# A new issue order for a fused attention and wave-MLP kernel, with 78 copies on other engines and filler products on TensorE

## The chip, the core and the metric

The kernel runs on one core of a Trainium2 chip. The metric is the device time of one execution in microseconds; three executions of the kernel before gave 228.94 (median), 229.01 and 228.08. A further execution was profiled, and all rows of the trace are from that one.

## What is computed

For each of 8 batches, 8 heads of 576 positions by 64 channels go through a linear attention with a root-mean-square norm, and the heads side by side (576 by 512) go through a wave MLP:

```python
kv = np.einsum('bhsd,bhse->bhde', k, v)
out = np.einsum('bhsd,bhde->bhse', q, kv)
x = out / np.sqrt(np.mean(out * out, axis=-1, keepdims=True) + 1e-06) * g_norm
theta = x @ w_theta                                   # x now (8, 576, 512)
y = w_tok_r @ (x * np.cos(theta)) + w_tok_i @ (x * np.sin(theta))
u = x + y
return u + np.maximum(u @ w_ch, 0.0)
```

Inputs and output are float32; the products run in float16 with sums in float32, but for batch 0's k-v product, which is taken in float32.

## The kernel before

A batch's 576 rows are cut into four full tiles of 128 rows (j = 0 to 3) and a tail of 64 rows, which is folded to 128 partitions by 256 columns (names ending in e). `plan()` (line 41) makes a list of 1205 numbered tasks, each with a kind, an engine and arguments; a string of numbers, `TURNS` (line 144), says in which order the tasks are issued, for all engines together. Each engine works through its own share strictly in that order, and semaphores that follow from the tiles' readers and writers make it wait. So `TURNS` sets two things: what stands behind what on each engine, and through this when a buffer comes free.

The tasks of one batch, in the order in which the data goes through them:

- **Loads.** `ldm` and `ldt` bring k and v (rows and tail) into three `stage` buffers in turn: batch 0's k has stage 0, its v stage 1, batch 1's k stage 2, batch 1's v stage 0 again. They are issued on SP (batch 0's v on ACT). `lq` and `lqe` bring q on POOL's queue, and its DMA casts to float16. `lw`, `lwe` (token weights, POOL), `lwth` (w_theta, SP) and `lwch` come once. `hold` (L331) is a copy of one element on POOL that waits until a part of k has landed, and so keeps back what POOL issues after it.
- **k-v product.** `ca` casts k and v to float16 (L365 on ACT for k, L367 on POOL for v); `kv` multiplies (L396; `kv32`, L377, for batch 0), `ko` copies the result into `kbd` (L269 on ACT, L273 on DVE).
- **Attention.** q is turned, for batches 0 and 1 on TensorE (`qt`, L412, and the copy `qo`), later by the DMA (`qd`, `qde`). `raw` is the product with `kbd` (L446, L455); `sq` squares on ACT (L466), `ss` sums on DVE (L475), `rt` takes the power -0.5 on POOL (L481), `x` scales on DVE (L493, L503).
- **Angle.** `xt` turns x on TensorE (L412), `xo` copies it out on ACT with the factor of g (L271), `th` multiplies with w_theta (L520, L527), `pt`, `arg`, `abs` reduce the angle (ACT L543, DVE L548, L555), `sin` and `cos` run on ACT (L563, L569), `z` multiplies on DVE (L583). `zmv` moves the tail's z on SP's queue (L589).
- **Token mixing.** `y` and `ye` multiply z with the turned token weights, in three parts (L605, L614). The weights are turned once, in nine tiles, by `wt` on TensorE (L352, L353) and copied out by `wo`; `wth` scales and casts w_theta.
- **Channel mixing.** `us`, `um` add x (DVE L619, L627), `ut` turns u (L412), `uo` copies it (L269), `v` multiplies with w_ch (L520, L527), `fin` joins both on DVE (L664), `st`, `ste` store on SP's queue.

TensorE's results stand in PSUM tiles of three tags: `tr` (two buffers) for what is turned, `raw` (two), `acc` (four) for the other products. Words of `TURNS` like `r18` are `idle(tag, n)` (L681): n filler products of 128 by 512 into a tile of that tag, whose result nobody reads. Before, there are two: `r18` and `r9`, both before 13 us.

Of the kernel before, what the change touches and what calls it, by code (L numbers as in the profile page):

```python
# [18 lines left out]
P = 128  # L19
# [125 lines left out]
5 1 8 0 4 9 r18 80 81 3 6 r9 66 67 16 52 44 53 2 45 7 13 12 46 47 11 15 68 69 14 73 59 54 55 70 71  # L145
72 48 56 74 49 60 50 57 34 51 30 10 82 35 38 83 31 58 26 84 39 186 61 62 19 85 27 42 18 36 17 63 86
43 64 75 40 37 65 76 28 22 24 41 29 184 183 32 77 25 33 78 123 21 23 187 124 96 97 87 125 88 79 126
127 190 98 189 193 99 185 114 115 105 188 100 106 89 191 194 200 90 199 197 128 101 91 116 196 107
192 92 195 102 117 337 103 336 108 104 93 204 338 198 205 201 94 118 119 202 129 211 203 232 95 109
206 212 218 130 207 213 120 131 214 121 208 136 110 111 209 233 480 140 215 216 481 122 137 139 135  # L150
210 112 134 225 234 113 219 226 133 346 217 487 235 236 145 141 132 220 339 493 239 240 248 249 146
237 150 151 20 142 335 496 221 351 238 138 275 155 144 222 276 157 147 490 143 152 149 154 342 343
340 227 356 349 345 348 148 277 158 241 344 278 242 153 223 352 279 174 483 347 224 228 159 243 350
280 175 250 353 281 229 354 251 160 252 230 253 482 164 156 244 231 161 166 355 282 165 283 245 176
357 341 359 360 257 358 286 369 258 285 246 254 266 484 167 361 267 362 169 162 370 259 287 284 260
247 177 255 488 491 179 371 363 372 268 625 489 261 256 494 262 492 626 269 263 180 292 170 291 497
270 364 264 501 373 374 495 265 272 365 290 271 273 366 274 498 367 502 375 627 500 368 296 295 376
628 301 485 393 377 499 297 306 384 394 486 302 307 379 385 395 300 380 386 168 381 382 308 309 378
411 396 638 310 383 289 305 412 387 420 514 504 515 397 294 402 288 388 516 299 517 505 293 506 503
389 507 304 421 422 390 298 399 635 518 509 398 403 391 510 629 171 303 163 511 178 508 316 311 318  # L160
512 423 424 636 400 519 404 632 317 426 642 326 633 312 392 425 405 639 331 513 524 630 172 427 319
321 320 413 525 526 173 327 770 520 646 406 414 332 323 322 521 415 634 637 538 640 529 428 641 527
407 539 643 324 408 522 328 528 313 409 565 530 644 645 416 329 523 431 401 430 540 566 541 314 567
547 556 568 417 429 569 542 531 548 570 418 771 432 434 437 419 571 435 410 647 772 557 532 773 572
442 649 544 533 650 330 436 651 535 439 916 447 573 777 780 652 631 444 783 774 440 654 543 655 325
449 534 653 445 433 452 536 576 574 648 441 656 454 545 438 455 657 575 182 537 786 446 546 450 658
781 549 550 778 181 659 915 451 784 443 660 683 787 664 448 665 918 577 551 674 684 558 661 675 553
779 666 471 782 559 461 315 785 472 560 552 662 473 788 463 917 453 466 476 791 789 663 667 790 462
669 554 474 676 477 561 670 464 562 668 677 582 456 563 457 555 671 467 685 468 678 692 672 564 932
928 923 578 693 775 776 673 587 469 679 592 583 710 792 597 701 588 686 919 680 687 681 688 694 580  # L170
682 711 689 599 695 712 702 690 713 593 714 600 581 585 929 691 931 794 715 465 586 696 922 590 591
799 697 795 800 796 716 334 703 595 698 579 797 793 596 801 475 458 924 802 798 804 584 717 718 704
925 805 705 699 803 806 621 926 707 589 594 927 828 930 819 333 933 829 700 706 807 598 814 808 1062
719 820 720 611 936 470 613 809 606 459 708 934 612 622 722 721 935 815 816 810 817 601 821 614 607
1063 811 830 822 602 812 818 616 608 855 460 617 831 727 823 825 618 856 709 832 939 732 857 737 824
937 479 813 1061 826 609 846 837 940 725 847 941 742 744 1068 848 730 858 827 942 619 834 838 944
735 859 849 943 921 861 850 860 1071 945 833 862 740 863 724 1060 851 949 946 864 1066 920 1065 729
723 734 1064 835 938 728 852 950 866 951 726 947 733 615 731 1074 948 624 1077 738 853 1067 865 1070
1069 1073 745 736 739 952 954 836 955 478 1072 964 1076 610 620 741 1075 973 956 957 867 839 1078
1083 1081 965 603 974 953 959 756 840 1079 966 841 761 1080 758 958 960 843 743 757 961 967 604 762  # L180
991 975 746 842 962 605 844 753 992 751 759 968 963 747 976 1000 854 970 845 977 1104 1082 872 766
752 1001 877 754 767 1105 1002 1003 882 982 1084 1106 887 969 993 1004 1005 979 983 1085 971 1086
994 889 1107 748 755 1108 972 984 1145 1006 890 1089 995 1007 978 1090 868 1146 871 980 1087 749
1091 981 1008 1092 985 1088 873 876 986 1093 878 1147 1094 881 996 888 997 1011 987 870 1095 883 998
# [549 lines left out]
```

## Time and profile before

| what | value |
|---|---|
| median of three runs | 228.94 us (228.08 to 229.01) |
| the profiled execution | 226.97 us; its span from first to last instruction 225.2 us |
| granted TensorE clock, mean | 0.939 |
| PE busy | 204.8 us in 1629 matmuls |
| DVE busy | 166.5 us in 318 instructions |
| ACT busy | 157.1 us in 304 instructions |
| POOL busy | 108.6 us in 115 instructions |
| DMA | 40.82 MB, 181 GB/s over the span |

The busy time of an engine is the union of its instructions' durations; PE overlaps matmuls, so its busy time says that something was in the array, not that it streamed at its peak. The granted clock is the share of the full TensorE clock. Times in the trace's rows count from the first instruction.

### The profile page before, as it was taken

The numbers are of one execution on the slowest core, as the hardware profiler recorded it, in microseconds if no ns is written. First come the engines' busy times: TensorE is split into PE (matmuls) and PEld (weight loads), VectorE is DVE, ScalarE is ACT, GpSimd is POOL, SyncE is SP. The second block draws the span as 40 slices with busy tenths as digits, with TensorE's granted clock in tenths as the row PEclk, the third lists the DMA queues.
The fourth block names the chain that finished last, engine by engine and source line by source line (L and its number), as shares of the span: only waits on it lengthen the run. The fifth ranks groups of instructions, "written<-read, shape, count | busy, mean of one in ns | idle before, by whom it ended". The sixth has DMA issues, their size and how long they took to land.

```text
span 225.2 us, 4427 instructions
## 1 busy us (share of the span) xinstructions
PE 204.8 (91%) x1629; PEld 115.3 (51%) x1629; DVE 166.5 (74%) x318; ACT 157.1 (70%) x304; POOL 108.6 (48%) x115
## 2 busy tenths in 40 slices
PE   7497879589997999989999998899999999999993
PEld 3166654445654554654565445454656455445451
DVE  5003854685799889997899689897998997776363
ACT  2014288998999688989779886889699666644130
POOL 8022567048678567930884288359734506001000
PEclk9955755969999999999999999999999999999999
DMA  5999699499999897999989979985991122204145
GB/s 141 229 229 169 210 311 192 154 300 249 169 273 140 215 243 204 188 242 209 274 139 316 215 110 249 257 250 39 255 172 51 66 78 82 70 3 151 47 171 190
DMA packets 63252, 40.82 MB, mean 181 GB/s; under 512 B 29312, under 2 KB 58624, under 8 KB 63232
## 3 DMA queue, kind: packets, MB, share of 16 engines
q1 hardware_dynamic: 47216, 32.81, 56.0%
q0 software_dynamic: 14432, 6.57, 23.7%
q10 hardware_dynamic: 1584, 1.18, 1.9%
q8 instruction: 12, 0.20, 0.4%
q14 instruction: 8, 0.07, 0.1%
HBM read 33.10 MB, written 9.44 MB: 189 GB/s over the span
## 4 chain that ended last, share of the span: by engine, by line
PE 44%; DVE 18%; ACT 13%; DMA 11%; POOL 8%; issue 3%; SPq 1%; POOLq 0%; DVEq 0%; ACTq 0%
PE y L605 14%; PE v L520 7%; PE th L520 7%; POOL rt L481 6%; DMA qh<-in_q_dram 5%; DVE ss L475 4%; DMA out_dram<-ot 3%; DMA stage<-in_k_dram 3%; DVE arg L548 3%; DVE x L493 2%; PE ups L412 2%; PE ye L614 2%; PE xps L412 2%; PE wps L352 2%; DVE kbd L273 2%
## 5 line engine op out<-in xcount | busy, mean ns | idle before, releaser
L481 POOL TENSOR_TENSOR rt<-ss,mhalf 128x8 f32<-128x8 f32 x32 | 53.9, 1686 | 54.6 <-DVE ss L475 52.5
L605 PE MATMUL y<-wT,zm 128*128 128x512 f16 x256 | 63.6, 382 | 0.6 <-DVE ote L664 0.3
L605 PEld LDWEIGHTS <-zm 128*128 128x128 f16 x256 | 23.8, 98 | 26.0 <-issue 2.6
L520 PE MATMUL th<-wth,xTb 128*128 128x512 f16 x128 | 33.8, 392 | 0.0
L520 PE MATMUL v<-wch,uTb 128*128 128x512 f16 x128 | 31.7, 379 | 0.0
L619 DVE SCALAR_TENSOR_TENSOR uTb<-y,gcol,xTb 128x512 f16<-128x512 f32 x32 | 23.3, 746 | 9.7 <-PE y L605 9.6
L493 DVE TENSOR_TENSOR x<-raw,rt 128x512 f16<-128x512 f32 x32 | 22.0, 688 | 10.0 <-POOL rt L481 9.7
L269 ACT COPY ur<-ups 128x512 f16<-128x512 f16 x32 | 18.4, 591 | 10.3 <-PE ups L412 9.4
L475 DVE TENSOR_REDUCE ss<-sqb 128x8 f32<-128x520 f32 x32 | 21.8, 689 | 4.7 <-ACT sqb L466 4.6
L271 ACT ACTIVATE xTb<-xps,gcol 128x512 f16<-128x512 f16 x32 | 21.3, 686 | 5.4 <-PE xps L412 2.7
L466 ACT ACTIVATE sqb<-raw 128x512 f32<-128x512 f32 x32 | 19.0, 596 | 8.5 <-PE raw L446 7.1
L548 DVE SCALAR_TENSOR_TENSOR arg<-pt,th 128x512 f32<-128x512 f32 x32 | 21.7, 682 | 4.0 <-ACT pt L543 3.8
L664 DVE SCALAR_TENSOR_TENSOR ot<-v,ur 128x512 f32<-128x512 f32 x32 | 21.7, 684 | 3.5 <-DMA out_dram<-ot 1.4
L569 ACT ACTIVATE sc<-arg,quarter 128x512 f16<-128x512 f32 x32 | 22.9, 723 | 1.9 <-DVE arg L555 1.8
L543 ACT ACTIVATE pt<-th 128x512 f32<-128x512 f32 x32 | 19.3, 604 | 7.1 <-PE th L520 7.0
L583 DVE TENSOR_TENSOR zm<-x,sc 128x1024 f16<-128x1024 f16 x32 | 21.6, 687 | 2.1 <-ACT sc L569 2.1
L367 POOL CAST v<-stage 128x640 f16<-128x640 f32 x28 | 19.5, 719 | 5.2 <-DMA stage<-in_v_dram 5.2
L563 ACT ACTIVATE sc<-arg 128x512 f16<-128x512 f32 x32 | 20.0, 633 | 0.5 <-DVE arg L548 0.4
L365 ACT CAST k<-stage 128x640 f16<-128x640 f32 x28 | 19.3, 726 | 0.2 <-DMA stage<-in_k_dram 0.2
L520 PEld LDWEIGHTS <-xTb 128*128 128x128 f16 x128 | 11.7, 100 | 11.6 <-issue 1.6
L520 PEld LDWEIGHTS <-uTb 128*128 128x128 f16 x128 | 11.6, 98 | 10.9 <-issue 0.4
L273 DVE CAST kbd<-kv 64x256 f16<-64x256 f32 (+1 forms) x18 | 7.0, 388 | 12.7 <-PE kv L377 12.6
(85 smaller groups left out, 310.6 us busy)
## 6 DMA issues: line engine op xcount, KB each, us to landing
out_dram<-ot SPq DMA_DIRECT2D x32, 256.0 KB, 2.8
stage<-in_k_dram SPq DMA_DIRECT2D x7, 1024.0 KB, 6.9
stage<-in_v_dram SPq DMA_DIRECT2D x7, 1024.0 KB, 7.7
qh<-in_q_dram POOLq DMA_DIRECT2D x7, 512.0 KB, 6.7
stage<-in_k_dram SPq DMA_DIRECT2D x2, 512.0 KB, 7.2
stage<-in_k_dram SPq DMA_DIRECT2D x8, 128.0 KB, 5.7
stage<-in_v_dram ACTq DMA_DIRECT2D x2, 512.0 KB, 9.6
zm<-in_moe_w_theta_dram SPq DMA_DIRECT2D x1, 1024.0 KB, 6.3
```

Of the source, the lines that this page charges most:

```text
L271: nc.scalar.activation(out=dst, in_=src, func=AFT.Copy, scale=by)
L475: nc.vector.reduce_sum(out=ss[:], in_=live.pop(("sq", b, j))[:], axis=AXX)
L481: nc.gpsimd.tensor_tensor(out=rt[:], in0=live.pop(("ss", b, j))[:], in1=mhalf[:, 0:h], op=ALU.pow)
L493: nc.vector.tensor_tensor(out=live["xp", b, p][:, :, a * HC:(a + 1) * HC].rearrange("p t (h e) -> p h t e", e=D), in0=r[:].rearrange("p (h ...
L520: nc.tensor.matmul(t[:], lhs(kc), w[:, kc, :], start=(kc == 0), stop=(kc == NKC - 1))
L548: nc.vector.scalar_tensor_tensor(out=arg[:, 0, :], in0=live.pop(("pt", b, j))[:], scalar=MAGIC, in1=live.pop(("th", b, j))[:], op0=ALU.sub ...
L563: nc.scalar.activation(out=sc[:, 1, :], in_=live["arg", b, j][:, 0, :], func=AFT.Sin, bias=0.0, scale=-TURN * SHRINK,)
L569: nc.scalar.activation(out=live["sc", b, j][:, 0, :], in_=live.pop(("arg", b, j))[:, 1, :], func=AFT.Sin, bias=quarter[:], scale=-TURN * S ...
L583: nc.vector.tensor_tensor(out=dst, in0=x.unsqueeze(1).broadcast_to((P, 2, w)), in1=sc[:], op=ALU.mult)
L605: nc.tensor.matmul(t[:], r[:, c * P:(c + 1) * P], wT[:, w, 0:SM], start=(w == 0), stop=(w == 2 * NJ))
L619: nc.vector.scalar_tensor_tensor(out=uTb[:, b % NUT, c, :].rearrange("p (j t) -> p j t", j=NJ), in0=live.pop(("y", b, c))[:].rearrange("p ...
L664: nc.vector.scalar_tensor_tensor(out=ot[:], in0=live.pop(("v", b, j))[:], scalar=0.0, in1=u[:], op0=ALU.max, op1=ALU.add,)
```

## The change

Three things change. First, all of `TURNS` is another order of the same 1205 tasks. Second, a word may end in A, D or P, which puts that task on ACT, DVE or POOL in place of the engine of `plan()`; 78 words do. From ACT to DVE go 19 `xo`, 7 `qo`, 7 `uo`/`uoe`, 5 casts of k, and 6 single ones (`wo`, `wth`, `ko`, `ko32`); from ACT to POOL 10 casts of k; from POOL to ACT 11 casts of v, to DVE 3; from DVE to ACT 7 `ko` (two copies each), one `ko32` and 2 `wo`. Third, there are more filler products: five words of the old kind (`r26`, `a8`, `a1`, `a1`, `r1`: 37 products of 128 by 512), and eight words `f` with 62 in all, which run into the tile that the next product is going to use: 15 ahead of batch 0's first k-v product, then 7, 6, 5, 16 ahead of `qt`, `wt`, `wt`, `xt` of the start, 2 (128 by 512) ahead of `th`, 5 ahead of batch 1's first `qt`, 6 ahead of an `xt` of batch 1. Ahead of a float16 tile a filler is a turn of 128 by 128; ahead of a float32 one it is a plain product.

```diff
 TURNS = """
-5 1 8 0 4 9 r18 80 81 3 6 r9 66 67 16 52 44 53 2 45 7 13 12 46 47 11 15 68 69 14 73 59 54 55 70 71
...
+2 1 3 4 17 5 16 r26 f15 48 49 0 44 10 6 52 66 7 45 53D 67D 8 f7 59 13 9 46A 73 50 47D 12 60D 80 54
+81 55 56 18 51D 68 14 69 15 57 74D 70 71 a8 f6 34 58 38 61 35 30 11 186 39A 72 19 a1 82 31 26 62 f5
...
     live = {}
+    lead = []
...
+    def ahead(at):
+        for _ in range(lead.pop() if lead else 0):
+            if at.dtype == FP16:
+                nc.tensor.transpose(at[:, 0:P], fill[:, 0:P], ident[:])
+            else:
+                nc.tensor.matmul(at, ident[:], fill[:, 0:at.shape[-1]], start=True, stop=True)
+
+    def bank(shape, dt, tag, n, name):
+        t = ps.tile(shape, dt, tag=tag, bufs=n, name=name)
+        ahead(t[:] if len(shape) == 2 else t[:].rearrange("p a b -> p (a b)"))
+        return t
...
-        t = ps.tile([P, S], FP16, tag="tr", bufs=2, name="wps")
+        t = bank([P, S], FP16, "tr", 2, "wps")
...
-            if word[0] in "ra":
+            if word[0] == "f":
+                lead.append(int(word[1:]))
+            elif word[0] in "ra":
                 idle({"r": "raw", "a": "acc"}[word[0]], int(word[1:]))
             else:
-                t = tasks[int(word)]
-                here["e_" + t.kind](t.eng, *t.args)
+                t = tasks[int(word.rstrip("ADP"))]
+                eng = {"A": "ACT", "D": "DVE", "P": "POOL"}.get(word[-1], t.eng)
+                here["e_" + t.kind](eng, *t.args)
```

All other tiles of PSUM are made by `bank` in the same way. Three places of the new order matter below. In the changed file a line stands 14 or 15 lines lower (18 in `e_ca`).

**SP, from its second load to the load of v of batch 1.** stage_64 is stage 0 (k of batch 0, then v of batch 1), stage_66 is stage 2, zm_81 takes w_theta. Before:

```order
L288 DMA stage_64<-in_k_dram 64x8x64
L319 DMA g_100<-in_g_norm_dram 128x64
L282 DMA stage_64<-in_k_dram 128x4x256
L288 DMA stage_64<-in_v_dram 64x8x64
L325 DMA zm_81<-in_moe_w_theta_dram 128x4x512
L322 DMA gcol<-in_g_norm_dram 64x1 x2
L288 DMA stage_66<-in_k_dram 64x8x64
L282 DMA stage_66<-in_k_dram 128x8x256
L282 DMA stage_64<-in_v_dram 128x8x256
```

Now:

```order
L302 DMA stage_64<-in_k_dram 64x8x64
L336 DMA gcol<-in_g_norm_dram 64x1
L333 DMA g_100<-in_g_norm_dram 128x64
L296 DMA stage_64<-in_k_dram 128x4x256
L336 DMA gcol<-in_g_norm_dram 64x1
L302 DMA stage_64<-in_v_dram 64x8x64
L339 DMA zm_81<-in_moe_w_theta_dram 128x4x512
L296 DMA stage_66<-in_k_dram 128x8x256
L302 DMA stage_66<-in_k_dram 64x8x64
L296 DMA stage_64<-in_v_dram 128x8x256
```

The row of v's tail, which needs stage 0 free, still stands ahead of w_theta. What moved is on the other engines: the last k-v product of batch 0, which frees stage 0, now stands on TensorE behind the turns of q's tiles 0 and 2; and k's heads 4 to 7 are loaded ahead of heads 0 to 3.

**POOL, its first loads.** qh and qe are q of batch 0, uTb is where the token weights are put. Before:

```order
L301 DMA qe_74<-in_q_dram 64x4x64 x2
L295 DMA qh_71<-in_q_dram 128x4x256 x2
L313 DMA uTb<-in_moe_w_tok_r_dram 64x576
L307 DMA uTb<-in_moe_w_tok_r_dram 128x4x576
L331 COPY gate<-stage_64 1x1
L313 DMA uTb<-in_moe_w_tok_i_dram 64x576
L307 DMA uTb<-in_moe_w_tok_i_dram 128x4x576
```

Now:

```order
L345 COPY gate<-stage_64 1x1
L309 DMA qh_71<-in_q_dram 128x4x256 x2
L315 DMA qe_74<-in_q_dram 64x4x64
L327 DMA uTb<-in_moe_w_tok_r_dram 64x576
L315 DMA qe_74<-in_q_dram 64x4x64
L321 DMA uTb<-in_moe_w_tok_r_dram 128x4x576
L321 DMA uTb<-in_moe_w_tok_i_dram 128x4x576
L327 DMA uTb<-in_moe_w_tok_i_dram 64x576
```

q and all token weights moved behind the copy that waits for k.

**DVE, from the first angle to the first z of a full tile of batch 0.** k_, v_ are the float16 copies of batch 1, zm and zf the z of batch 0. Before:

```order
L548 SCALAR_TENSOR_TENSOR arge<-pte,th 128x256
L548 SCALAR_TENSOR_TENSOR arg<-pt,th 128x512
L555 TENSOR_SCALAR arge<-arge 128x256
L555 TENSOR_SCALAR arg<-arg 128x512
L548 SCALAR_TENSOR_TENSOR arg<-pt,th 128x512
L555 TENSOR_SCALAR arg<-arg 128x512
L583 TENSOR_TENSOR zm_79<-x,sc 128x1024
```

Now:

```order
L383 CAST k_68<-stage_66 128x640
L508 TENSOR_TENSOR x<-raw,rt 128x4x2x64
L570 TENSOR_SCALAR arg<-arg 128x512
L563 SCALAR_TENSOR_TENSOR arg<-pt,th 128x512
L570 TENSOR_SCALAR arg<-arg 128x512
L563 SCALAR_TENSOR_TENSOR arge<-pte,th 128x256
L289 TENSOR_SCALAR xTb_85<-xps,gcol 128x512
L383 CAST v_70<-stage_64 128x640 x2
L570 TENSOR_SCALAR arge<-arge 128x256
L383 CAST v_70<-stage_64 128x640
L598 TENSOR_TENSOR zm_79<-x,sc 128x1024
```

One cast of k, three of v and a copy of a turned tile came onto DVE here; each stands between the angle and z.

60 lines of the change are left out of this document (52 added, 8 removed), and 55 rows, old and new, of the table TURNS.

## The prediction, on record before the run

> **What bounds the kernel now.** I read the page's busy tenths first, then two stretches of the span, then the chain and the timelines inside the first 50 us. The tenths of TensorE, its granted clock and the DMA over 40 slices of 5.6 us:
>
> ```profile
> PE   7497879589997999989999998899999999999993
> PEclk9955755969999999999999999999999999999999
> DMA  5999699499999897999989979985991122204145
> ```
>
> From slice 13 on TensorE is nearly always busy at the full clock; before that it has holes, and the clock is mostly at half. The busy times cut at the first token-mixing product, with columns PE, PEld, DVE, ACT, POOL, then clock, DMA share and GB/s:
>
> ```profile
> 0.00:47.50 47.50, 36.00 (x284) 22.68 (x285) 20.13 (x48) 24.21 (x48) 18.98 (x29) 0.73 0.90 207
> 47.50:222.00 174.50, 168.81 (x1348) 92.60 (x1346) 146.09 (x271) 132.88 (x258) 89.57 (x86) 1.00 0.80 174
> 60.00:180.00 120.00, 114.85 (x971) 64.88 (x970) 108.06 (x206) 102.34 (x201) 74.03 (x72) 1.00 0.96 194
> ```
>
> After 47.5 us TensorE is idle for 174.5 - 168.8 = 5.7 us only. So the kernel is a start of 47.5 us, in which 284 of 1629 matmuls run, and a rest bound by TensorE; moving the start forward by one microsecond moves the end by about one, as long as the others keep up. DVE comes closest: in 60 to 180 us it is busy 108.1 of 120, idle 11.9.
>
> In the start, these rows of SP's and TensorE's timelines and of SP's waits say what comes when:
>
> ```profile
> SPq L288 <- PE kv L377: 15.9, 1, 15.9
> 22.74 0.62 SPq L325 DMA_DIRECT2D zm<-in_moe_w_theta_dram  x1
> 19.90 2.13 PE L377 MATMUL kv<-stage,stage 128*64 128x64 f32 x40
> 30.07 0.62 PE L352 MATMUL wps<-ident,uTb 128*128 128x128 f16 x4
> 30.87 0.58 PE L352 MATMUL wps<-ident,uTb 128*128 128x128 f16 x4
> 34.05 1.06 PE L527 MATMUL th<-wth,xTe 128*64 128x256 f16 x8
> 47.50 1.72 PE L605 MATMUL y<-wT,zm 128*128 128x512 f16 x4
> ```
>
> SP stands 15.9 us until batch 0's last k-v product (to 22.03) frees a stage buffer; only then is w_theta asked for, at 22.74. The nine weight tiles are turned until 31, the angle product begins at 34.05, the first y at 47.50.
>
> **The loads of the start.** Times from issue to landing, and POOL's wait and a later load of q:
>
> ```profile
> zm<-in_moe_w_theta_dram SPq DMA_DIRECT2D x1, 1024.0 KB, 6.3
> uTb<-in_moe_w_tok_i_dram POOLq DMA_DIRECT2D x1, 576.0 KB, 9.1
> uTb<-in_moe_w_tok_r_dram POOLq DMA_DIRECT2D x1, 576.0 KB, 14.8
> qh<-in_q_dram POOLq DMA_DIRECT2D x1, 512.0 KB, 5.9
> stage<-in_k_dram SPq DMA_DIRECT2D x2, 512.0 KB, 7.2
> 2.71 0.43 SPq L282 DMA_DIRECT2D stage<-in_k_dram  x1
> 13.16 0.18 POOL L331 COPY gate<-stage 1x1 f32<-1x1 f32 x1 [7.47 <-DMA stage<-in_k_dram]
> 13.83 0.76 POOL L307 DMA_DIRECT2D uTb<-in_moe_w_tok_i_dram  x1
> 33.35 0.94 POOL L295 DMA_DIRECT2D qh<-in_q_dram  x1
> ```
>
> Now k and v go alone and q waits for them. Before, the gate opened at 13.16 with q and one weight beside these loads. k's second half, issued at 2.71 then and one issue of 0.6 us later now, would land at 10.5 with the 7.2 us of such a half; between 10.5 and 13.2 I take 12.1. q (512 KB, 5.9 us) is then whole at 18 and its first half about a microsecond earlier; two turns of it and the last k-v product end at 18, against 22.03. w_theta is asked for at 18.6 instead of 22.74 and lands, with 6.3 us and one more for the weights beside it, at 26 instead of 29.
>
> The token weights pay for that. They are issued behind four loads of q, some 0.76 us each, and the small weight tail: tok_i at 17.4 instead of 13.83. With its 9.1 us it lands at 26.5, with tok_r's 14.8 us at 32.2; I take the first, its own row, and keep the second as an end. Four of the nine tiles need tok_r alone and are turned by then; five remain at 30.87 - 30.07 = 0.80 us each, to 30.5. With a turn of x and its copy (0.7 us, row below) the angle product begins at 31.3, against 34.05: 2.8 us earlier.
>
> From there to the first y it was 47.50 - 34.05 = 13.45 us. Two things end it now. POOL asks for batch 1's q after `rt` of tile 3, whose `raw` stands right behind the first turn of x: 31 + 0.60 + 0.69 + 1.69 for square, sum and power gives 34, as the load did at 33.35 before; with 5.9 us q is there at 40, its two turns at 41. And the z of tiles 0 and 1, which ACT makes:
>
> ```profile
> L365 ACT CAST k<-stage 128x640 f16<-128x640 f32 x28 | 19.3, 726 | 0.2 <-DMA stage<-in_k_dram 0.2
> L271 ACT ACTIVATE xTb<-xps,gcol 128x512 f16<-128x512 f16 x32 | 21.3, 686 | 5.4 <-PE xps L412 2.7 <-DVE uTb L619 2.6
> L466 ACT ACTIVATE sqb<-raw 128x512 f32<-128x512 f32 x32 | 19.0, 596 | 8.5 <-PE raw L446 7.1 <-issue 1.1
> L475 DVE TENSOR_REDUCE ss<-sqb 128x8 f32<-128x520 f32 x32 | 21.8, 689 | 4.7 <-ACT sqb L466 4.6
> L481 POOL TENSOR_TENSOR rt<-ss,mhalf 128x8 f32<-128x8 f32 x32 | 53.9, 1686 | 54.6 <-DVE ss L475 52.5 <-DVE g L335 2.1
> 45.11 0.68 DVE L583 TENSOR_TENSOR zm<-x,sc 128x1024 f16<-128x1024 f16 x1
> ```
>
> Before, the second z ended at 45.8, 11.75 us after the first angle product, with four casts of k on ACT in between. Two of these are gone from ACT, 2 x 0.73 = 1.5 us: 31.3 + 10.2 = 41.5. Both paths meet there, so the first y comes at **41.5 instead of 47.5: 6.0 us gained**. Against it: batch 1's first two `raw` and two turns, which stood ahead of the first y, now stand behind it, about 0.8 us at full clock; and the fillers behind it (6 turns and one product), at most 6 x 0.06 us (eight turns took 0.45 us at full clock, row below) and 0.22 us (half of the 1.72 / 4 of the half-clock y above), 0.55 us in all where no hole takes them:
>
> ```profile
> 202.57 0.45 PE ups L412 x8
> ```
>
> All earlier fillers stand ahead of something that TensorE must wait for in any case, which hides them: the flight of q and the weights from 12 to 26 us and the copies behind each turn. With that cover gone, `a8`, `a1`, `a1` and the other 56 of `f` would cost up to 10 x 0.43 + 56 x 0.11, some 10 us at half clock. Net of the start: -6.0 + 0.8 + 0.55 = **-4.7 us**.
>
> **The clock.** Whether the fillers lift the clock is a matter of what they are. Stretches of one clock window each, TensorE alone (busy, clock), and the weight turns in 25 to 35 us:
>
> ```profile
> 25.00:28.41 3.41, 3.41 (x24) 0.50 0.85 282
> 28.41:31.82 3.41, 3.22 (x23) 0.50 1.04 306
> 35.24:38.65 3.41, 3.41 (x15) 0.50 1.31 165
> 25.00:35.24 10.24, 5.37 (x36) 1.26 (x3) 2.54 (x4) 0.50 1.00 309
> ```
>
> Two windows with 3.41 and 3.22 us of work, mostly turns, left the clock at half; after the third, with `th` in it, it was full. 45 of the 62 new fillers are turns. My 0.80 us for a weight tile is a half-clock spacing, so I credit the fillers with nothing. The Trainium skill ("TensorE: Matmul & The Clock Gate", Part 4: PE-mode transpose) says that a turn by identity does not count as TensorE work for the clock gate; it speaks against most of the new fillers, and the two rows agree. By that rule the sum stays at -4.7; if turns counted, it would be -6.7 (the third rival).
>
> **The 78 copies.** Durations: ACT's cast 0.73 and turned copy 0.69 from above, and
>
> ```profile
> L367 POOL CAST v<-stage 128x640 f16<-128x640 f32 x28 | 19.5, 719 | 5.2 <-DMA stage<-in_v_dram 5.2
> L269 ACT COPY ur<-ups 128x512 f16<-128x512 f16 x32 | 18.4, 591 | 10.3 <-PE ups L412 9.4 <-DVE ot L664 0.9
> L269 ACT CAST kbd<-kv 64x256 f16<-64x256 f32 x14 | 5.1, 365 | 3.3 <-DVE kbd L273 3.2
> L273 DVE CAST kbd<-kv 64x256 f16<-64x256 f32 x14 | 5.8, 417 | 0.1
> L275 DVE TENSOR_SCALAR wth<-zm 128x512 f16<-128x512 f32 x2 | 0.8, 420 | 0.0
> L555 DVE TENSOR_SCALAR arge<-arge 128x256 int32<-128x256 int32 x8 | 2.7, 342 | 0.1
> ```
>
> No row shows DVE casting 640 elements or copying a turned tile with a factor; the nearest is 420 ns for 512, so 0.42 for the copy (up to ACT's 0.69) and 0.53 to 0.73 for the cast. Behind the first y, DVE gets 13 full `xo` (5.5), 4 tail ones (1.4), 4 casts (2.4), 5 `uo` and 2 `qo` (2.8), 2 `uoe` (0.7), 2 `ko` (1.7) and gives 7 `ko` (14 x 0.417 = 5.8): **+8.7 us**. ACT loses 13 casts, 13 + 4 `xo`, the `uo`, `uoe`, `qo` and 2 `ko`, gains 11 casts and 7 `ko`: about -14 us. POOL changes by 9 x 0.72 - 11 x 0.72 = -1.4. DVE has 28.4 us of idle time after 47.5 and ACT 41.6, so I take **0**, and keep as ends -5.7 (all of TensorE's idle time after the first y gone) and +8.7 (all of DVE's added work passed on).
>
> Sum: the profiled execution took 226.97 us (1.8 above its span), so 226.97 - 4.7 = 222.3; against the median of 228.94, which lies 2.0 higher, **224.2 us**.
>
> **The rivals.** DVE's waits between 60 and 180 us begin with this row:
>
> ```profile
> DVE x L493 <- POOL rt L481: 3.5, 6, 1.5
> ```
>
> - *DVE becomes the bound.* Place: 60 to 180 us, where DVE idles 11.9 us, in small waits for POOL, ACT and stores that more work need not fill; the largest group there is 3.5 us in six waits. Turned tiles would wait for their copy behind DVE's sums and scalings, and `th` behind them. Price: all of the 8.7 us, so 228.94 - 4.7 + 8.7 = 232.9. It decides the sign once more than 4.7 + 1.1 = 5.8 of the 8.7 us go through. For it: 90% busy in that stretch. Against it: ACT, which is as often on the chain, loses 14 us. Chance 0.23.
> - *The start gains nothing.* If tok_i takes 14.8 us as tok_r did, it lands at 32.2, the angle product begins at 37, later than now, and only DVE's and ACT's lighter start brings y back to about 47: 228.9. For it: SP's loads of w_theta, k and v then run beside the weights. Against it: SP's and POOL's queues ran side by side before 13 us too. Chance 0.10. That q and the weights are late is also how the change could fail to do what it says: the fillers then fill waits that it made itself.
> - *The fillers hold the clock, and the new order closes holes.* The five weight tiles at 0.5 us save 1.5, `th` at full clock half a microsecond more: -6.7; and if half of TensorE's 5.7 us of later idle time goes, -9.5: 219.4. Against it: the clock rows above. Chance 0.22.
>
> **How the numbers follow.** Forecast 0.45, with its own range 221 to 227.5 from the ends of the gate and the weights. The range to hold 8 in 10 reaches into the first and third rival: 218.5 to 232. A measurement of this kernel can tell about 0.5%, 1.1 us, from no change. Faster by more than that: the forecast but for its upper edge and the third rival, 0.66; within it, the second rival, 0.10; slower, the first, 0.24 with a little of the second.
>
> **What would show it.** Right: SP issues w_theta near 18.6 us; the last weight tile is turned near 30, the first y near 41.5; TensorE's idle time behind it is 4 to 8 us. Wrong: tok_i landing after 30; the clock full between 25 and 35 us; DVE over 95% busy between 55 and 175 us with waits of TensorE on L289; an end of TensorE that moves by less than the first y does.

## The result and the profile after

| what | before | after |
|---|---|---|
| median | 228.51 us (4 runs beside the change: 227.00 to 229.01) | 240.03 us (4 runs: 238.78 to 241.99) |
| ratio | | 1.0523, interval 1.0435 to 1.0612 |
| the profiled execution | 226.97 us, span 225.2 us | 238.78 us, span 237.0 us |
| first y begins | 47.50 us | 47.01 us |
| from there to the end of the span | 177.7 us | 190.0 us |
| PE, DVE, ACT, POOL busy | 204.8, 166.5, 157.1, 108.6 us | 208.9, 177.4, 142.2, 107.2 us |

Ratios, here and below, leave out executions that took over 1.5% longer than the fastest of the same kernel.

The change makes the kernel slower by 12.0 us (0.0523 x 228.51), where 4.7 us of gain were forecast. In the profiled executions the first y comes 0.5 us earlier, and all that follows takes 12.3 us longer. The tenths of the page, 40 slices of 5.9 us, answer to those of before:

```profile
PE   7948499986965989999879999999799999999993
PEclk9997858999995899999999999999999999999999
DMA  6899980989798869997999999979854022303325
```

TensorE has new holes between 53 and 77 us, and the clock falls between 71 and 83 us, where it was full before. The busy times cut at the same places (PE, PEld, DVE, ACT, POOL, then clock, DMA share and GB/s):

```profile
0.00:47.01 47.01, 37.60 (x335) 23.20 (x335) 22.28 (x56) 17.14 (x32) 18.39 (x28) 0.85 0.84 178
...
60.00:180.00 120.00, 108.72 (x927) 62.90 (x926) 104.22 (x201) 92.73 (x183) 74.05 (x72) 0.97 0.95 198
...
47.50:222.00 174.50, 159.73 (x1299) 90.05 (x1298) 146.93 (x284) 122.87 (x240) 88.79 (x83) 0.98 0.78 174
```

Behind 47.5 us TensorE is now idle for 174.5 - 159.7 = 14.8 us, against 5.7. Between 60 and 180 us DVE is busy for 104.2 us, less than the 108.1 of before, although it does 177.4 - 166.5 = 10.9 us more in all. So DVE is not full there.

**The start.** SP's and TensorE's timelines of after at the places that the prediction named:

```profile
17.90 0.95 SPq L339 DMA_DIRECT2D zm<-in_moe_w_theta_dram  x1
...
22.67 0.25 PE L366 MATMUL wps<-ident,uTb 128*128 128x128 f16 x1
26.37 0.36 PE L366 MATMUL wps<-ident,uTb 128*128 128x128 f16 x3 [3.46 <-DMA uTb<-in_moe_w_tok_i_dram]
...
34.77 0.62 PE L366 MATMUL wps<-ident,uTb 128*128 128x128 f16 x4
...
37.59 1.15 PE L535 MATMUL th<-wth,xTb 128*128 128x512 f16 x4
...
47.01 1.04 PE L620 MATMUL y<-wT,zm 128*128 128x512 f16 x4
```

The first weight tile gets one turn as soon as tok_r is there, and its second turn waits 3.46 us for tok_i: here no tile could be turned from tok_r alone. The timeline of before had shown the same, and I read past it:

```profile
22.94 0.36 PE L352 MATMUL wps<-ident,uTb 128*128 128x128 f16 x3 [0.72 <-DMA uTb<-in_moe_w_tok_i_dram]
```

Both weights lie interleaved in one buffer, and the wait for the second is set for reads of the first too. So the later tok_i (landed at 26.3 us, as foreseen) held back all nine tiles; the last is turned at 35.5 us, the angle product begins at 37.59, later than before (34.05). Only the shorter way from there to the first y (9.4 us instead of 13.45) brings the start back to even; ACT is busy for 8.2 us of it (before 12.1), while DVE has more work than before, 8.3 us (7.4). The wait has a second price: TensorE was busy for 1.2 of the 3.4 us up to 27.6 us, and from there to 37.8 us its clock stood at half.

**Behind the first y.** The two kernels between 50 and 80 us, first before, then after:

```profile
50.00:60.00 10.00, 10.00 (x84) 5.31 (x83) 6.41 (x11) 8.97 (x16) 9.36 (x11) 1.00 1.14 230
60.00:70.00 10.00, 9.26 (x86) 5.63 (x85) 9.34 (x18) 9.45 (x21) 5.62 (x6) 1.00 1.15 201
70.00:80.00 10.00, 8.90 (x83) 5.09 (x82) 8.85 (x18) 7.45 (x14) 7.40 (x9) 1.00 1.01 191
```

```profile
50.00:60.00 10.00, 7.64 (x59) 3.69 (x57) 6.23 (x11) 4.02 (x8) 4.43 (x4) 1.00 1.13 307
60.00:70.00 10.00, 8.17 (x89) 5.56 (x87) 8.95 (x18) 9.55 (x21) 9.51 (x11) 1.00 0.93 142
70.00:80.00 10.00, 6.94 (x35) 3.56 (x34) 4.76 (x11) 3.05 (x7) 0.00 (x0) 0.66 1.17 189
```

TensorE's busy time is 28.2 us in these 30 us before and 22.8 after, some of it at a lower clock. What stands behind it is in the timelines, first SP's and POOL's of before:

```profile
41.04 0.37 SPq L282 DMA_DIRECT2D stage<-in_v_dram  x1
...
48.41 3.31 POOL L481 TENSOR_TENSOR rt<-ss,mhalf 128x8 f32<-128x8 f32 x2 [9.66 <-DVE ss L475]
...
54.90 0.80 POOL L328 DMA_DIRECT2D wch<-in_moe_w_ch_dram  x1
```

then SP's, POOL's and TensorE's of after:

```profile
46.94 0.59 SPq L296 DMA_DIRECT2D stage<-in_k_dram  x1
...
51.03 0.59 SPq L296 DMA_DIRECT2D stage<-in_v_dram  x1
...
53.18 1.66 POOL L496 TENSOR_TENSOR rt<-ss,mhalf 128x8 f32<-128x8 f32 x1 [8.69 <-DVE ss L490]
...
59.54 1.38 POOL L381 CAST v<-stage 128x640 f16<-128x640 f32 x2 [1.22 <-DMA stage<-in_v_dram]
...
63.47 0.79 POOL L342 DMA_DIRECT2D wch<-in_moe_w_ch_dram  x1
...
50.52 2.75 PE L620 MATMUL y<-wT,zm 128*128 128x512 f16 x12
...
56.20 0.47 PE L629 MATMUL ye<-zt,wT 128*64 128x256 f16 x2 [2.36 <-DMA zt<-zf]
...
73.55 1.06 PE L542 MATMUL v<-wch,uTe 128*64 128x256 f16 x8 [2.53 <-DMA wch<-in_moe_w_ch_dram]
```

It reads as a chain. v of batch 2 is asked for at 51.03, behind k of batch 2 and the four moves of the tail's z (before at 41.04). POOL's cast of it starts at 59.54; behind that cast, on POOL's queue, stand q of batch 2 and then w_ch, at 63.47 (before at 54.90). w_ch takes 10.0 us instead of 7.5, lands at 73.5, and the first channel product v waits 2.53 us for it. But POOL waits only 1.22 us for v there. Its first `rt` behind the first y, which needs DVE's sum, starts at 53.18 instead of 48.41, and between it and w_ch stand three casts instead of one. Whether v's lateness is a link of the chain at all is what e2 tries.

To count how far TensorE gets, I take each product of the trace that is not a filler at its spacing at full clock: 12 y in the 2.75 us above are (2.75 - 0.38) / 11 = 0.215 us per 512 columns (0.38 us is the duration of a single one), the others by their columns (the tail's products of 256 columns, which run in pairs, at half). All of the kernel's products come to 169.7 us. What has begun by a given time, in one execution of each kernel:

| time, us | before | after | e1_wch | e3_split | e14_old_start | e17_to_first_y_split |
|---|---|---|---|---|---|---|
| 50 | 14.4 | 13.7 | 14.4 | 17.2 | 13.9 | 13.6 |
| 60 | 23.8 | 20.6 | 21.8 | 22.5 | 22.5 | 21.8 |
| 80 | 39.7 | 31.4 | 36.0 | 36.6 | 36.0 | 37.7 |
| 120 | 75.7 | 65.6 | 69.7 | 69.6 | 70.6 | 73.9 |
| 200 | 149.1 | 137.4 | 142.6 | 143.1 | 142.6 | 147.2 |

After is 8.3 us behind at 80 us and 11.7 at 200 us. Differences of about 1 us say nothing: e14 has the order of before, word for word, up to about 75 us, and at 60 us it is 1.3 us behind before.

### The profile page after: what moved, and what is told of

Read it like the earlier page. It is cut to its first block, busy times and chain, and to the rows that moved or that the text cites. A ratio compares the mean times of both kernels' runs of the same rounds, so it can differ in the third digit from the quotient of the medians.

```text
span 237.0 us, 4579 instructions
## 1 busy us (share of the span) xinstructions
PE 208.9 (88%) x1701; PEld 118.8 (50%) x1701; DVE 177.4 (75%) x351; ACT 142.2 (60%) x275; POOL 107.2 (45%) x111
## 3 DMA queue, kind: packets, MB, share of 16 engines
q0 software_dynamic: 14432, 6.57, 22.7%
## 4 chain that ended last, share of the span: by engine, by line
PE 35%; DMA 26%; DVE 16%; POOL 8%; SPq 5%; ACT 4%; issue 4%; DVEq 0%; POOLq 0%; ACTq 0%
DMA stage<-in_v_dram 11%; PE y L620 10%; PE v L535 8%; PE th L535 5%; DMA uTb<-in_moe_w_tok_i_dram 4%; DMA wch<-in_moe_w_ch_dram 4%; POOL rt L496 4%; DMA stage<-in_k_dram 3%; DVE ot L679 2%; DVE ss L490 2%; PE wps L366 2%; PE ups L427 2%; DVE uTb L634 2%; DMA qDD<-qh 2%; DVE arg L563 2%
## 5 line engine op out<-in xcount | busy, mean ns | idle before, releaser
L620 PE MATMUL y<-wT,zm 128*128 128x512 f16 x256 | 62.8, 379 | 0.3 <-DVE arg L563 0.2
L535 PE MATMUL v<-wch,uTb 128*128 128x512 f16 x128 | 33.6, 395 | 0.0
L535 PE MATMUL th<-wth,xTb 128*128 128x512 f16 x128 | 32.6, 380 | 0.6 <-DVE xTb L289 0.3
L558 ACT ACTIVATE pt<-th 128x512 f32<-128x512 f32 x32 | 19.1, 599 | 11.7 <-PE th L535 11.4
L283 ACT COPY ur<-ups 128x512 f16<-128x512 f16 x27 | 15.8, 589 | 14.5 <-PE ups L427 13.7
L283 ACT CAST kbd<-kv 64x256 f16<-64x256 f32 (+1 forms) x26 | 9.3, 357 | 15.7 <-PE kv L391 15.0
L285 ACT ACTIVATE xTb<-xps,gcol 128x512 f16<-128x512 f16 x18 | 12.3, 692 | 5.5 <-DVE uTb L634 3.2
L648 POOL TENSOR_TENSOR uge<-ue,g 128x256 f32<-128x256 f16 x8 | 5.5, 682 | 21.5 <-DVE ue L642 21.5
L411 PE MATMUL kv<-v,k 128*128 128x128 f16 x140 | 11.9, 219 | 3.1 <-POOL rt L496 1.6
## 6 DMA issues: line engine op xcount, KB each, us to landing
zm<-in_moe_w_theta_dram SPq DMA_DIRECT2D x1, 1024.0 KB, 11.5
```

Of the source, the lines that this page charges most:

```text
L283: nc.scalar.copy(out=dst, in_=src)
L535: nc.tensor.matmul(t[:], lhs(kc), w[:, kc, :], start=(kc == 0), stop=(kc == NKC - 1))
L620: nc.tensor.matmul(t[:], r[:, c * P:(c + 1) * P], wT[:, w, 0:SM], start=(w == 0), stop=(w == 2 * NJ))
```

## The experiments

Three theories went in. **L**: the loss is in late loads of the new order, tok_i for the weight tiles and v of batch 2 and w_ch behind the first y. **D**: it is in the copies on other engines. **F**: it is in the fillers. Unless said otherwise a kernel is the changed one with one edit; ratios are to the kernel before on the same chip, and the microseconds beside them are the ratio times that kernel's median there (228.1 to 229.1).

### One load, one buffer, or the fillers

**e1_wch**: w_ch (word 20) is asked for right behind q of batch 1.

```diff
-78 98 187 88 99
+78 98 187 20 88 99
...
-159 251 20 222 230
+159 251 222 230
```

> Only the load of w_ch is moved, on POOL's queue from behind the casts of batch 2's v (issued at 63.5 us) to right behind batch 1's q (about 41 us). Theory L (late loads: batch 2's v and w_ch are asked for late and TensorE runs out of work between 50 and 80 us): the 2.5 us wait of v for w_ch at 71 to 73.5 us and the half clock after it go, time 235 to 237 against 240.0. Rival D (VectorE, which got the copies, is the bound) and rival F (the fillers cost the time): within 1.5 us of 240.

Measured: 1.0226 (1.0017 to 1.0436), +5.2 us. The wait for w_ch is gone, and the first v begins here:

```profile
69.57 0.63 PE L542 MATMUL v<-wch,uTe 128*64 128x256 f16 x8
```

By the ratios this one load gives back 6.8 of the 12.0 us, by the medians (234.62 against 240.03 us) 5.4 of 11.5; the interval is wide (0.4 to 10.0 us of loss left).

**e2_v2**: all four loads of batch 2 (335 to 338) ahead of the moves of the tail's z (135 and on).

```diff
-189 201 135 f5 211 335 204 95 108 132 338 117
+189 201 335 336 337 338 135 f5 211 204 95 108 132 117
```

> Only the four loads of batch 2's k and v are moved on SP, from behind the moves of the tail's z (v at 51.0 us) to ahead of them. Theory L: v of batch 2 lands at about 52 instead of 59.4 us, w_ch behind its casts is asked for some 7 us earlier, and the time falls to 231 to 235. Rival D and rival F: within 1.5 us of 240.

Measured: 1.0370 (1.0195 to 1.0544), +8.5 us. That is more than theory L had (231 to 235), though 2 us less than after by the medians. v of batch 2 landed at 52.0 us instead of 59.4 and POOL waited for no load, yet w_ch was asked for only 0.8 us earlier:

```profile
54.86 1.66 POOL L496 TENSOR_TENSOR rt<-ss,mhalf 128x8 f32<-128x8 f32 x1 [8.69 <-DVE ss L490]
...
62.68 0.79 POOL L342 DMA_DIRECT2D wch<-in_moe_w_ch_dram  x1
```

It landed at 71.5, and TensorE still waited 1.32 us for it. So v's lateness is not what holds w_ch back: what stands ahead of it on POOL does, an `rt` that waits for DVE and the casts behind it. The moves of the tail's z kept TensorE waiting no more. The first y came at 48.68 here and at 47.01 in after, although the words up to there are the same in both: two executions of one start can lie 1.7 us apart.

**e3_split**: each token weight has a contiguous half of the buffer.

```diff
-    wn = room[:, 0:2 * NJ * S].rearrange("p (j s) -> p j s", j=NJ)
+    wn = [room[:, i * NJ * S:(i + 1) * NJ * S].rearrange("p (j s) -> p j s", j=NJ) for i in range(2)]
...
-            out=wn[:, :, i * S:(i + 1) * S],
+            out=wn[i],
...
-                nc.tensor.transpose(t[rows, jj * P:(jj + 1) * P], wn[:, jj, cols], ident[:])
+                nc.tensor.transpose(t[rows, jj * P:(jj + 1) * P], wn[i][:, jj, cols], ident[:])
```

> Each token weight gets its own contiguous half of the buffer, so that turning tok_r need not wait for tok_i. Theory L: the four tiles of tok_r alone are turned before 26.5 us, the last weight tile before 33 instead of 35.6, the first y 2 to 3 us earlier; but the stretch from 50 to 80 us still waits for v and w_ch, so the time falls by 0 to 3 us, 237 to 240. Rivals D and F: the first y comes earlier as well, the time stays within 1 us of 240.

Measured: 1.0229 (1.0001 to 1.0457), +5.2 us. TensorE's timeline:

```profile
31.00 0.38 PE L365 MATMUL wps<-ident,uTb 128*128 128x128 f16 x4
...
43.18 1.04 PE L619 MATMUL y<-wT,zm 128*128 128x512 f16 x4
...
52.69 0.47 PE L628 MATMUL ye<-zt,wT 128*64 128x256 f16 x2 [2.67 <-DMA zt<-zf]
```

The last weight tile is turned at 31.5 us and the first y comes at 43.18; the prediction had 30.5 and 41.5. The 3.8 us gained on after have three parts that the edit does not separate. The wait is gone; tok_i also landed earlier, at 24.5 us instead of 26.3 (with the halves the page counts 13664 packets on the queue of POOL's loads, q0, instead of 14432); and the clock stayed full through the weight turns, so that the nine tiles took 7.3 us instead of 9.2:

```profile
26.14:29.56 3.42, 3.26 (x39) 2.32 (x37) 2.60 (x7) 1.04 (x3) 0.72 (x3) 1.00 1.08 357
```

That the buffer took most of the start's gain does not rest on this one trace: with one buffer the first y comes at 46.0 to 48.7 us in all seven traces in which it stands at this place of the new order (after, e1, e2, e4, e5, e10, e15), with halves at 42.8 to 45.3 in all three (e3, e7, e11). The time is better than theory L had it (237 to 240). But the 3.5 us of products gained by 50 us are down to 1.9 by 60 us, in the wait for the tail's z above, behind k of batch 2.

**e4_nofill**: no fillers but `r26`.

```diff
-2 1 3 4 17 5 16 r26 f15 48 49 0 44 10 6 52 66 7 45 53D 67D 8 f7 59
+2 1 3 4 17 5 16 r26 48 49 0 44 10 6 52 66 7 45 53D 67D 8 59
```

> All fillers but the first 26 are taken out (62 of the new kind and 11 of the old). Rival F: they cost TensorE time, 235 to 237. Theory L and rival D: nothing that matters, 239 to 241; the granted clock before 38 us loses at most one window of 3.4 us.

Measured: 1.0376 (1.0202 to 1.0550), +8.6 us, first y at 46.0. The tenths of the clock:

```profile
PEclk9987556999967999999799999999999999999999
```

The clock is lower up to 40 us, and the kernel is no slower for it: the fillers bring nothing that shows. By the ratios it is 3.4 us faster than after, by the medians 2.0, between F's 235 to 237 us and the 239 to 241 of L and D; the intervals overlap, so a cost of the fillers of a few us is not excluded. F falls as the main cause.

### The copies

**e5_engines**: the new order with all suffixes taken off, so that the 78 copies run where they ran before.

```diff
-52 66 7 45 53D 67D 8 f7 59 13 9 46A 73 50 47D
+52 66 7 45 53 67 8 f7 59 13 9 46 73 50 47
```

> The new order with its fillers, but all 78 copies and casts on the engines they had before. Rival D (VectorE became the bound): DVE loses some 11 us of work and the time falls to 232 to 235. Theory L (late loads): the late requests stay and ScalarE gets 15 us of work back, so 240 to 246.

Measured: 1.1120 (1.0958 to 1.1283), +25.6 us. The chain's shares by engine:

```profile
PE 35%; DMA 18%; ACT 17%; DVE 10%; POOL 10%; SPq 5%; issue 4%; POOLq 0%; ACTq 0%; DVEq 0%
```

ACT is 17% of the chain; in after it is 4%. Neither theory had so much (D 232 to 235 us, L 240 to 246). The copies' new engines are worth 25.6 - 12.0 = 13.6 us to the new order: order and engines belong together, and neither can be priced without the other.

**e6_before_copies**: the old order with the 78 suffixes.

```diff
-70 71 72 48 56 74 49 60 50
+70 71 72 48 56 74D 49 60D 50
```

> The old order without any new filler, but with the 78 copies and casts on their new engines. Rival D: the added 11 us on DVE show here as well, 233 to 237 against 228.5. Theory L: the loads keep their old places, so the copies alone cost little, 227 to 231.

Measured: 1.0423 (1.0379 to 1.0466), +9.7 us. At 50 us it is ahead of before (16.7 us of products against 14.4; the first y comes at 44.99 us), at 70 us even (31.9 against 32.3), at 200 us 9.9 us behind. DVE is the third busy time here:

```profile
60.00:180.00 120.00, 107.31 (x905) 60.11 (x904) 103.16 (x199) 88.14 (x175) 67.86 (x66) 0.99 0.90 190
```

With all its added work DVE is busy for 103.2 of 120 us. The copies cost this order 9.7 us without any engine being full, so D holds as "the copies cost" on the old order, and not as the rival of the prediction had it, by a full DVE.

**e12_before_xo** and **e13_before_casts** take the old order with only the 19 `xo`, and with only the 29 casts, on their new engines.

```diff
-184 183 32 77 25 33 78 123 21 23 187 124
+184 183 32 77 25 33 78 123 21 23 187 124D
```

> The old order, with only the 19 copies of turned x moved from ScalarE to VectorE. All 78 cost 9 us there, with VectorE no busier than before between 60 and 180 us. If it is the copies of turned x, that the angle product now waits for behind VectorE's queue: 231 to 235. If it is the casts of k and v that change places: within 1.5 us of 228.5.

```diff
-127 190 98 189 193 99 185
+127 190 98 189 193D 99 185
```

> The old order, with only the 29 casts of k and v on their new engines (11 of v from POOL to ACT, 10 of k from ACT to POOL, 8 to VectorE). If the casts cost the 9 us, by keeping the loads' buffers and the engines' queues waiting for a DMA: 231 to 236. If the copies of turned x do: 227.5 to 230.

Measured: 1.0128 (1.0058 to 1.0198) and 1.0178 (1.0121 to 1.0235), +2.9 and +4.1 us. Both conditions on record came true in part: together these are 7.0 of the 9.7 us, and the other 30 copies had no run of their own. The largest wait of TensorE behind 60 us in e12:

```profile
103.72 0.63 PE L541 MATMUL th<-wth,xTe 128*64 128x256 f16 x8 [2.18 <-DVE xTe L288]
```

and in e13 the same kind of wait, with what stood ahead of it on ACT:

```profile
129.36 0.72 ACT L378 CAST v<-stage 128x640 f16<-128x640 f32 x1 [5.04 <-DMA stage<-in_v_dram]
129.99 0.68 ACT L284 ACTIVATE xTb<-xps,gcol 128x512 f16<-128x512 f16 x1
...
130.72 0.58 PE L426 MATMUL xps<-ident,x 128*128 128x128 f16 x4 [3.23 <-ACT xTb L284]
```

This is how a copy costs more than its duration. The cast of v, moved to ACT, stands 5.04 us until v has landed; the copy of a turned tile is queued behind it, and TensorE waits 3.23 us for that copy. At 120 us e13 is less than 1 us behind before in products, at 150 us it is 4.6 us behind. In before, POOL waited for v 5.2 us in all, and TensorE waited 0.4 us for POOL's casts.

### The loads put together

**e7_repair** is e1, e2 and e3 at once; **e8_before_split** is the old kernel with e3's buffer. Their edits are those above.

> The new order with three repairs together: the split token weights, batch 2's k and v loaded ahead of the moves of the tail's z, and w_ch right behind batch 1's q. Theory L: the first y at about 43 to 44 us, v of batch 2 landed by 51, no wait for w_ch, so all of the loss of 11.5 us of which 3.5 stand before 60 us and some 6 more before 90 us comes back: 227 to 231. Rival D: the start gains 3 us and w_ch's wait goes, but DVE holds the middle: 232 to 236.

> The kernel before, with only the token weights in two contiguous halves. tok_r landed at 19.7 us and tok_i at 22.9 us there; if the first weight tile waits for tok_i through the overlap of the interleaved halves, it now begins up to 3 us earlier, but w_theta (29.0 us) and the order of the tiles still hold the angle product: 226 to 228.5. If the wait was for tok_r itself: 228.5 within 1 us.

Measured: e7 1.0386 (1.0212 to 1.0561), +8.8 us, worse than e1 or e3 alone at their medians and outside what L and D had (227 to 231, 232 to 236). It has one wait more than those:

```profile
50.54 0.37 PE L426 MATMUL qps<-ident,qe 128*128 128x128 f16 x2 [4.17 <-DMA qe<-in_q_dram]
```

The tail of q of batch 1 now stands behind w_ch and beside v of batch 2. e8: 1.0037 (0.9993 to 1.0081), no difference that can be told: the old order asks for tok_i early, and there the interleaved buffer costs nothing that shows.

**e10_queue** puts v of batch 2 ahead of the z moves, k of batch 2 behind them, and w_ch behind the first tail of q of batch 2; **e11_queue_split** adds e3's buffer.

```diff
-189 201 135 f5
+189 201 337 338 135 f5
...
-134 133 121
+134 133 335 336 121
...
-206 340 225
+206 340 20 225
```

> The new order with three moves among the DMA requests only: batch 2's v ahead of the four moves of the tail's z on SP, batch 2's k behind them (these moves waited behind a 1 MB load, TensorE stood 2.4 us for them), and w_ch behind the three small q loads on POOL, not ahead of them as in the run that repaired three things and gained a wait for q. Theory L: the first y stays near 46.5 us, TensorE's waits for z's tail and w_ch go, 230 to 233. Rival D: 235 to 238.

> The same moves and the split token weights. Theory L: the first y at 43 to 44 us as in the split alone, and the stretch up to 80 us as full as before: 227 to 230. Rival D: 233 to 236.

Measured: e10's two runs, 237.01 and 241.71 us, lie too far apart for a ratio; both miss L's 230 to 233, and the first lies within D's 235 to 238. e11 1.0317 (1.0255 to 1.0378), +7.3 us, far from L's 227 to 230. Its median of 236.05 us is near the 233 to 236 of rival D, but DVE is not full (busy 107.5 of 120 us between 60 and 180). The first y comes at 42.8 us, and now k is late:

```profile
58.48 0.44 PE L410 MATMUL kv<-v,k 128*128 128x128 f16 x5 [3.82 <-ACT v L378]
```

ACT's cast of v stands behind its cast of k, which waits for k of batch 2 (asked for from 44.7 us on, its last part landed at 56.5). After, e3, e7 and e11 have their largest waits between 50 and 74 us for four different transfers (w_ch, the tail's z, q's tail, k): moving a request there chooses what is late.

### Which part of the order

**e14_old_start** has the first 300 words of the old order, to about 75 us, and then the rest in the new order (45 copies moved); **e15_new_start** the reverse (32 copies moved). The seams:

```diff
 169 162 370 259 287
-284 260 247 177
+170 486 255 179
```

> The first 300 words of the old order (to about 75 us: first y, the loads of k2, v2, w_ch, the first products v), on the engines of plan(), and then every other task in the order and on the engines of the change (46 of its 78 copies). Theory L (the loads between 36 and 75 us are late in the new order, and that is most of the loss): the early loss is gone and what the trace of after showed behind 80 us, about 3 us, stays: 231.5 us, 230 to 233. Rival R (the order behind 75 us with its copies on DVE is most of it, and what looked like a late start would have been made good by the old order behind it): 234 us or more.

```diff
 166 357 246 256 369 493
-370 359 180 258D
+175 176 359 360
```

> The first 300 words of the new order with their engines and fillers (to about 75 us), and then every other task in the old order on the engines of plan(). Theory L: 8 of the 11.5 us remain: 236.5 us, 235 to 238. Rival R: 231 to 233 us, since the old order behind 75 us has TensorE idle time that a late start can use.

Measured: e14 1.0152 (1.0055 to 1.0248), +3.5 us; e15 1.0442 (1.0318 to 1.0566), +10.1 us. The two add up to 13.6 us, the whole change costs 12.0 (9.9 to 14.0): most of the loss is made in the first 75 us and stays, a quarter is made behind. By the ratios e14 is 232.6 and e15 239.2 us, so L's 231.5 and 236.5 were 1.1 and 2.7 us too low; rival R, with 231 to 233 for e15, is out. In e14 TensorE waits for DVE, at the seam (74.23 us) and at 164.42 us:

```profile
PE y L620 <- DVE zm L598: 2.2, 1, 2.2
PE kv L411 <- DVE uTb L634: 2.0, 1, 2.0
```

In before TensorE's y waits 0.2 us for zm in all, and its kv not at all for uTb.

**e16_to_first_y** takes only the first 147 words of the new order, which end ahead of the first y and of the loads in question (18 copies moved), and then the old order; **e17_to_first_y_split** adds e3's buffer.

```diff
 131 94 198 189 201
-135 f5 211 335 204
+117 337 336 108 204
```

> The first 147 words of the new order with their engines (18 copies) and fillers, which end behind batch 1's loads of k, v and q and just ahead of the first y and of the loads of k and v of batch 2 and of w_ch; then the old order on the engines of plan(). Theory L: the first y comes at about 47 us as in both kernels, the loads of batch 2 and w_ch come as in the old order, v2 landing near 48 and w_ch near 63: 228.5 us, 227 to 230. Rival R2 (the new start itself, with q of batch 1 and the weights late, costs what comes behind it): 232 us or more.

> e16 with each token weight in a contiguous half of its buffer, so that four weight tiles wait for tok_r alone. Theory L: the first y comes near 43 us as in e3_split and the loads behind it are those of the old order: 224.5 us, 223 to 227, the four microseconds that the prediction of the start counted. Rival B (the DMA is full between 36 and 60 us, so that batch 2's loads and w_ch set the pace whenever the first y comes): first y near 43, but 228 us or more, with new waits of TensorE for kv or wch between 48 and 65 us.

Measured: e16 1.0115 (1.0029 to 1.0200), +2.6 us, between L's 227 to 230 us and R2's 232; e17 0.9972 (0.9930 to 1.0014), 0.6 us less, which is not to be told from nothing. So the new start, up to the first y, costs 2.6 us of e15's 10.1; words 148 to 300 cost the other 7.5. They hold the requests of batch 2 and w_ch and 14 copies, and no run separates these. The last wait ahead of the first y, in e16:

```profile
48.08 0.37 PE L426 MATMUL qps<-ident,qe 128*128 128x128 f16 x2 [3.49 <-DMA qe<-in_q_dram]
```

and in e17, with the first y itself:

```profile
47.22 0.27 PE L425 MATMUL qps<-ident,qe 128*128 128x128 f16 x2 [2.61 <-ACT kbd L282]
...
48.29 1.83 PE L618 MATMUL y<-wT,zm 128*128 128x512 f16 x4
```

L's 224.5 us for e17 fell. In the old order the first y stands behind the turn of q's tail of batch 1, so it could not come earlier. Nor did the halves bring anything up to the angle product here (35.34 us, in e16 35.41): TensorE came to the first weight tile at 26.0 us in e17 and at 25.5 in e16, when tok_i was as good as there (26.1 and 26.3). Hence a last run.

**e18_y_first** is e17 with z of tile 0 (95) and the first two y (136, 137) ahead of that turn (232).

```diff
-201 117 337 336 108 204
+201 95 117 337 336 108 204
...
-203 232
+203 136 137 232
```

> e17 with the product of z of batch 0's tile 0 and its first two y moved ahead of the turn of q's tail of batch 1, where TensorE stood idle for 2.6 us. If the place of the first y was all that hid the gain of the start (theory L): first y at about 44.7 us instead of 48.3, two y of 0.9 us each fill the hole, 227 us (1.5 to 2 us below e17), 225.5 to 228. Rival B (DMA sets the pace behind it): the first y comes earlier all the same, but the time stays at that of e17, 228.5 us, 227.5 to 230, with TensorE waiting for loads or stage buffers further on.

Measured: 1.0127 (1.0084 to 1.0170), +2.9 us. The first y does come 3.1 us earlier than in e17:

```profile
45.17 1.90 PE L618 MATMUL y<-wT,zm 128*128 128x512 f16 x8 [0.34 <-DVE zm L596]
```

By 50 us 15.5 us of products are done, 1.9 more than in e17; by 60 us it is 22.0 against 21.8, by 70 us 30.3 in both. The lead goes in small waits (0.9 us for the tail's z is the largest), as rival B had it for the first 20 us. That e18 then ends slower than e17 B did not foresee, and no run settles it.

No kernel here is faster than the one before by more than its interval. e17 comes nearest.

## Why the prediction was wrong

- **Gate, q and w_theta's request.** Right: the gate opened at 11.5 us (12.1 taken), q's halves landed at 15.8 and 18.0 (17 and 18), w_theta was asked for at 17.9 (18.6). Its duration was mis-sized: it landed at 29.4 and not 26, after 11.5 us and not 7.3; the weights and k and v of batch 1 were on their way at the same time, but no run isolates that. It held nothing up, the angle product began at 37.6.
- **"Four of nine tiles need tok_r alone and are turned by then."** This is the step of the start that failed. tok_i landed at 26.3 us, near the 26.5 of the forecast, and that was luck: it was asked for 1.7 us earlier than forecast and took 10.6 us instead of 9.1. But all nine tiles waited for it, and the last was turned at 35.5 and not 30.5 us. e3 took that wait away, and the first y came at 43.2, near the 41.5 of the forecast; it got there partly at a full clock, which the forecast had not counted on. The row of before that tells it was in the trace (22.94, with its wait for tok_i).
- **From the angle product to the first y.** Right: 9.4 us (10.2 taken, 13.45 before), and as forecast the second z (done at 46.95) and the turns of q (46.9) meet just ahead of the first y. Net, the start gained 0.5 us and not 6.0, no more than executions differ by.
- **"So I take 0" behind the first y.** This is the step that failed by more: it was 12.3 us (190.0 - 177.7), outside the ends of -5.7 and +8.7. The work that it counted was there: DVE has 8.8 us more behind the first y (155.1 against 146.3). But the step weighed the copies by how full each engine is, and fullness was not the matter: DVE was less busy between 60 and 180 us than before. What the step did not price is what stands behind what. The order up to 75 us makes most of the loss (e15, +10.1), three quarters of it in the words behind the first y (e15 less e16, 7.5), where v of batch 2 is asked for at 51.0 instead of 41.0 us and w_ch at 63.5 instead of 54.9; the order and copies behind 75 us make the rest (e14, +3.5). That the requests are what costs in these words is shown for w_ch alone (e1, 6.8 us by the ratios, with a wide interval). e3 gives back as much, and the two together with e2 only 3.2 (e7): the parts do not add, what is left moves from load to load, and no run gives it all back with the new order kept. How much of the 7.5 us is the 14 copies' stays open.
- **The copies' durations.** DVE's casts of k took 0.81 us, more than the range given (0.53 to 0.73), its turned copies 0.48, a little more than was taken (0.42). ACT lost 7.8 us of work behind the first y (132.9 to 125.1) and not 14:

```profile
L383 DVE CAST k<-stage 128x640 f16<-128x640 f32 x5 | 4.0, 809 | 0.0
...
L289 DVE TENSOR_SCALAR xTb<-xps,gcol 128x512 f16<-128x512 f16 x14 | 6.7, 477 | 0.3 <-PE xps L427 0.3
```

- **The fillers and the clock.** Right to credit them with nothing (e4). A stretch of 3.41 us in the start, in which TensorE is busy throughout and does nothing but turns, left the clock at half; it was full from 37.8 us on, just after the angle product had begun:

```profile
30.92:34.33 3.41, 3.40 (x25) 2.29 (x24) 1.17 (x4) 1.28 (x2) 2.61 (x2) 0.50 1.02 287
```

  The Trainium skill ("TensorE: Matmul & The Clock Gate", Part 4: PE-mode transpose) says that a turn does not count as busy for the gate as other products do, and that the full clock does not engage for it; this row agrees that turns do not lift the clock. e3 shows the other side: its row above, 30 turns among 39 matmuls, began at the full clock and kept it.
- **The rivals.** That the start gains nothing came true, by another way than tok_i landing at 32 us. "DVE becomes the bound" had the sign, but not the mechanism (DVE busy 104.2 of 120 us) nor the size (232.9). The fillers holding the clock did not happen in after (half from 27.6 to 37.8 us). No rival had what decided: an order behind the first y that leaves TensorE waiting with no engine full.

## What to carry to other kernels

When an order of issue changes, follow every load to its request: what stands ahead of it on the queue that issues it, and what that in turn waits for; busy shares, even 90%, say neither that there is room nor that there is none. A copy moved to another engine costs what it makes wait behind it, so look for the engine whose queue has nothing urgent behind a wait for DMA. And before counting on data that lands first, look in the trace whether its reader really starts then: a shared, interleaved buffer can tie it to the last load.

## What the runs showed of the hardware

A small move asked for behind a large load can take as long as the load. Of the tail's z moves of after (32 KB each) the one issued at 46.37 us, ahead of k's 1 MB, and the one issued at 47.57, behind it, took, in us from issue to landing:

```profile
zt<-zf SPq DMA_DIRECT2D x1, 32.0 KB, 1.8
...
stage<-in_k_dram SPq DMA_DIRECT2D x1, 1024.0 KB, 5.9
zt<-zf SPq DMA_DIRECT2D x1, 32.0 KB, 5.6
```

It landed 0.3 us after k; whether their queue or the full DMA (share 1.13 between 50 and 60 us) held it, no run tells.

The same load can take much longer in another order; in after, where w_theta took 6.3 and w_ch 7.5 us before:

```profile
zm<-in_moe_w_theta_dram SPq DMA_DIRECT2D x1, 1024.0 KB, 11.5
...
wch<-in_moe_w_ch_dram POOLq DMA_DIRECT2D x1, 512.0 KB, 10.0
```

And DVE's cast of k takes 809 ns where its cast of v, of the same size, takes 538 ns (811 and 484 in e13). The cast of k also changes the order of its elements (`p h j d` to `p j h d` in `e_ca`), that of v does not; no run tells whether that is why.

The clock can keep either state through a stretch that is mostly turns: half in after (30.92 to 34.33 us), full in e3 (26.14 to 29.56 us).
